# Turning eight kept rows of h by transposing DMAs instead of on TensorE, with a new order of all instructions

## The chip, the cores and the metric

The kernel runs on one core of a Trainium2 chip. The metric is the device time of one execution in microseconds (us); a time "of the runs" is the median of separate executions. One execution was also recorded by the hardware profiler, and everything said of engines, waits and transfers comes from that record. Engines are named as the profile names them: PE (TensorE: matmuls and transposes), DVE (VectorE), ACT (ScalarE), POOL (GpSimd) and SP (the engine that issues the DMAs here).

## The reference

A layer with a forward pass and its gradients, in bfloat16, with S = 2048 tokens, D = 512 channels and F = 1376 hidden features. Cut to what matters:

```python
xn  = layernorm(A_q)
kv  = shift_conv(k, shift_k) * v                  # four taps along the tokens
y   = causal_conv(kv, ssm_k) + kv * ssm_D         # convolution over all 2048 tokens, by FFT
mlp = ((xn @ w_gate) * (xn @ w_up)) @ w_down      # no nonlinearity: a bilinear GLU
out = A_q + xn * y + mlp
# result: out, and the gradients of out with respect to A_q, k, v, shift_k,
# ssm_k, ssm_D, w_gate, w_up, w_down for the given grad_out
```

With g = xn @ w_gate, u = xn @ w_up and d = grad_out @ w_down^T, the bilinear part needs three products per token and hidden feature: g·u (for the output and for w_down's gradient) and d·u, d·g (for the gradients of w_gate, w_up and xn). In the kernel these three are called **h**. Each h is needed twice and in two layouts: with tokens on the partitions for the weight gradients, and with features on the partitions, that is transposed, for the output and for the gradient of xn.

## The kernel before, in words

**Tiling.** The 2048 tokens are R = 16 rows of 128 tokens. Features are cut into NST = 6 stages j of 256 columns, stage 1 being only 96 wide (L26). `mlp_rows` (L402) makes h for one stage and two rows: matmuls into PSUM, copies by ACT and DVE, and products by DVE. It writes them to a ring in SBUF of RING = 28 slots; a slot of 1536 bytes per partition holds the three h of one row and one stage, that is 128 partitions by 768 bf16 values. `slot(j, r)` (L273) gives the address. Stage 4's rows 0 to 15 lie in slots 0 to 15 and stage 5's in 16 to 27 and 0 to 3.

**From rows to features.** `hd_store` (L429) stores h to a DRAM tensor HD, and `hd_load` (L616) later loads one pair of rows back through a transposing DMA, into one of two buffers of SBUF, `hdP[n % 2]`. It is one DMA per row pair n = 0 to 7: 1152 rows by 768 columns for n < 4 and 896 rows by 768 columns for n = 4 to 7. The second is smaller because the last KEEP = 8 rows of stage 4, like all 16 rows of stage 5, are never stored: they stay in the ring ("kept rows") and are turned in place. `turn_gen` (L593) does that: 24 kept rows of 6 blocks of 128x128 each are 144 transposes on PE, eight at a time into PSUM, and each eight are copied back over the slot by one ACT COPY of 128x1024. `hd_block(m, t, fb)` (L620) tells the matmuls where the transposed block fb of row m lies: in a loaded buffer or in a ring slot.

**Stages of time.** The MLP stages run first, together with `dw_gen` (L568: the weight gradients of a finished stage, matmuls over its ring rows) and `a_gen` (L439: first step of the long convolution). Then `s_gen` (L550) does the middle of the convolution through the DRAM tensors AX and CX, beside the last weight gradients. From about 275 us on comes what is called the **F part** here, a loop over the eight row pairs n: `c_load` (L650) brings 1.5 MB of CX, `last_dft` (L691), `c_dkv`, `c_y`, `c_o5`, `c_dsk` and `dk_pair` finish the convolution and its gradients, mostly on DVE; `y_o` (L756) and `y_x` (L773) are the groups of 11 and 22 matmuls of 128x512 per row that read the transposed h and give the output and the gradient of xn. `hd_load(n + 2)` fills the buffer that the groups of pair n read last.

**Order.** Nothing runs in the order of the Python text. Every call on an engine is recorded as an operation (the helper at L173 then issues it, so that nearly every instruction of the profile has the line L173), and `emit` (L181) replays them in an order unpacked from the string PLAN, which also names a PSUM bank for every buffer. This string sets each engine's order, and SP's: all DMAs are issued from SP into one hardware queue, in PLAN's order. An SP instruction that waits holds up all DMAs behind it. The DMAs share eight semaphores in turn, so that each also waits for the one eight places before it.

Of the kernel before, what the change touches and what calls it, by code (L numbers as in the profile page):

```python
# [10 lines left out]
BF = mybir.dt.bfloat16  # L11
# [6 lines left out]
S = 2048  # L18
D = 512
F = 1376  # L20
R = 16
NFB = 11
NST = 6
# [5 lines left out]
KEEP = 8  # L29
RING = 28  # L30
RO = [0, 16, 24, 40, 56, 72]
EPS = 1e-5
PLAN = "c-lQzbrhFHu$`WzyBq0lBn0Ucl<rOmLFtwTC8a?^q`O1u?v@To=|(}~{qVi>&bPbY?CjlhXXc-sn-Kt#07EfI0P!IyB!qY%P!tkDW+)B{1`fF(86<`PQ6MVhhG-BSQov^r15!auNDi?eHXwWsai9d0f;><fN<vD=52>L5bb`205XwOrNCV}eEL4EJ@F^66e9!<sf$H!K3d3{w3K~H*aIFC~p$Qa$T2KdCLuY6SJ)sRWgvwAGDneuE4RxUxjDc401q_Bt&=l%HCYTIEpbw0KW>6m%LthBm7Dhuq7z<rs0BnKg@HO;@b}$9T!4mi$+Cvri76!sr=m1$@5Uhi}kQUNIM_2><AS+abTsR(P!#6M$et~o_4Ss_4uok|9=`aE2z+A`)8z47sgyFCWy21$P26^yTm;sxiJ4}S3Fb@{Mm+%`*f}deN41-&c3SYtt$cw+jD;Nn&VL2>=g)kE`z~8U}Rzfs92#a7p`~%w{A0C1O@B{3C!|)nX<4(8$X>dCnfozZ#Kfz0o1M=f8NQZA=H=Kl3kRCH&Mmz=aFcY4Jb5H=^!f`kcXW$~7fPWz~{sEUE3!a7BkQM)g=y)As;0<^W*)Tiagkz8ct7A?qh&Aw2tcil}pb*By!dMGyV=TM_vGEGjLB%3i7Y&PIJ*<z8E#NPRgG+G<eul+x85YL|_&I)n78n=fV@tdWt#CQ6hA6lKTVoqUY>N#M@Gk7YuW=<d!eQ7B+aqBIY>dNk72bm%Apv&8Z?F?a#YET{o8V5|g$Z#tHpOqT8ScRmxEB-SefSQiVOM+rBa!h3d<fleH8#he@JAelQ}7Y2#V0TtyWlu{3^Q;#PQdZF27kuxxCp1>7#xceu_R8y9#{hRVRq<=y)X%`!&2BAH(+Tz3WKN&_QAerx)J+ffBXdp(*RtLzv68C9_QdpyiILr2+hTSWpN-L#CbRf=VLi6j|*@cwxyvoj0WQnOp3{II90&Lv>#_-GOUPAsUc0J5j2esU<zzTm2f(>qDIt&T2pgcj4kMEYDb-^2OPq0X$DosqxcPdfj`q>tb#{yCRN2Ru@ilTDRCAZ$7+~}64M#{1J7a-`kv0=dAxuZF)1aZOL!TR(-mw_SMeJDiL>b>rl9M13V);<*nn>0LOeyc@HXDTzwj=0pp-O_PT)OEMW^XLo}tu~h92NUe1wnj4|;-|@hLvTp?H>_;}(2@FYy)rjcMs0e2s7LUz`PR@g2U$4+wOEkUpW`Fdd~Qq71|&q|}EBQAMgmg((vmITfLzl$qvGpvshmveG%qMxRj>ib};O8WpFEbPPYI67&UCp{n#HeMKdy6qTmF6rHM38Hz!_V|E%z=P4#tryLZE%2I6FgmLHx+K%NYF2$pqv=#4AeEN%OP%g?%lj$xcpz?GYCu1JUOZliK)uP%|hw4%V%1`&G9?hi!RFFQU?`R&)rykUWex+X2jk?k*>P<aq6s@K))Sp(+SXxgTX%F<Hm9&gT(+0Xvn`kYKr{%PUcF|9?nI_T>x=7>bH=01ZX$ozlowSg)(|cM%59keDgGsc7_R=D{K#OS){Y!7@cltnw=^dS<Kj{eVC*&J+lLk;sK0piT5nU(XhZLJ*@l!ZRariMEq9?@sl(te%&c)9tHy@>?B%FtjQC`l+m*^_x=POizFH=GOl$`??;==rbUQtR;#YMO%f5v~)Eh@$@DK$T*=zNWoV{kkk$BEduI7j7wC@x3gk^BQE;h~&>6LV4?&QUZCkKm}9kcaU;O3rEdM@~qiI2nJ!#OZiEm*6S<6PM(vJdLaIbgs_nIRj_pOgw>Wa9oY2@pT6O%q=N1N7I@-iED9mjiE7h442|8oRv#+EFH_)IJRcz+FXX`aao?o2{ew*<-}Tt%W--Bh3ZoUuE>eBBmK%rwJzu2N}N!WXcw->$+a@q=lT2vXVtFUjjM12&Ze&^nWoU}no?8i9Inb=a$5b0b7*(Ypba^l{=%uW5$Do0nqGTwPVLE`Xk*T;y|@WC<viM(7jj0O#m%@6_vO5rS^IH+E~J?>i#F#0{5`keQd&e?ax2cK3%IZj<j;8!7u9t%nAdYjEvBt`1GnL}{58+y&$N~<;o4eO+i`xaqf5Cx7tqqWj63kB+L60c8Lgltw4kQoa#~3nXnFmHmvcjHq#L;tU*pcag8$^}TwK4<P5doa)s<XVzvCNxlPhX<ea5%AvewhD^h>?X&-o75)E4>|*Vnt;Qa{(#e2-W0eSW|Xxs^WRD*Bi^YEyl}jr9dr(;E7%HrJQ@iqlI5$tcaVwRY0u)Ir;5CizC=^LLtAhVa+=H+RwB_#b}FUA3FG*DTUj+v)e(L*MWq%_>dwUw+F2wX<fE?DCF>>3bfbJNN_VkZlZ-Q*uc(9<JSWu=dh^x|311a~~b5xn+R%)-60ldn!p^9jT+akZk4Myo(D<9vP!WWHI;GsX9gT$_y<iV>O?Q(_?&`i^_QYRPxJOUdNxwPdY(Q@JZgxKkHImuH|Hzp5oK|qn_bExV%i)X*x=0X)zhCGxaR*=h=FY5AZoY#6Rc?U8(V9j#iRibd^?+^L&Ia@LXN3lewZy*0p+(FY#W!%#~%LuF-j#Kv;g&gtABzNn%-`3w0ka(cQX1CutQ)BC|QEh!mGix>2w2dQB#aHMv~nEt*0Ob6wf1^YwE%sM|E9Y}GGho$k{5l1l2yW^Ev;Mdf!*Bc&v*{HBNX6WOCBq_phUbh1wm=w&S_NA-|4l0AG?O|EEdDI?ppj<{UV9eP}Y9MMZ!Riem6J)y_+tTvRga!R90G&!y3^eLaw^IBcLk{WVdtI0{dp=-FiT+^HSrSy<?(puWfEp020^o~ZCo>Eg{$RB!JW6BeaC9&nPzR;cewX~6^`cnVWT5?xk=~3<_%_WZ9(~i<qddo8<Yaz`fuKcObmEa$3EMoVyk93f}@<#uZe!><{u8Ud|`CDJB+k5?2`^#0iCO2e&nElSdZpu@MVqhQi8@VmF<eh#mZ#9uU(1FrY21!&yi*DaZD|se^C59!jnATZ_NEi85;#y+sB#-5e#J3OfMB-UDS;R?gs1%T{azsFfNi2(F(d?ndwxe=iQdn~POO8n@yDO*<WSZo#ly*;YT0%>0&t<y2kX)9`j>`#|AzAHbNo(2cq@=T%a!O818vDc&*h85m*)6?gv<ya?*>c+%$!oJEk3Ev&_J^F6b8=qtSqaNztof~g&5;Z8i_Ddaa!Cr>uad>)$*1<Y&6fqTP!>rcyKiOep<R}e_F78Yzw*Eq%kT153fpkmB4w?djga#8w-mLJ@`DtyA7zw`maS6E#>i*3O~y(^D`n$kygauG_JwVi%J!2~vI(+7zO;!lNhZrTwo`UV6?-F7WVckaS|(c6mPj4@NA}2G*(dwufE<)Va#%W9XIm;?*)o|bwXLo#mwL8BUdgw%QtI1x*2SvZOIanWrK@$bnzlyvS$C^pbFGoRu*SAl8d?)uC;P2|HMM58UN*=(X>L92iEWgg_Qnp_3F~F=<yU)bo8*WcwBGi}`q(^cVMk51ueG#RHs6j}YinZ*Y`krjw${(SwsyAA7THPr$tGBP>u(dSgZ(Cx?6^&~j<(pA*c4l8FHQW4Otob;&8FLOTVd|6>~DK*-`fluXkYnL8x)aJKigo7<1_6a`(Q(Ct<AEPHq@f{FjJpx>uiqwVux(Kt+Lg2*f!X3dv7Cbr2SwUZIeB-%@+KW{b&R1HydSZESjIT-))PHHukNy&BoYv8*4jkr;W2+h92E_+a62hF+8=ui?mreJdMZn{BEAi|FyJ!*<$+{`@@oZ0#E1#JcXz9PrRBJ^mM-0u2?pIYl%FuC-GQb*gy63UePOgQjhA@J*Q{zhF-*r`e&Zq3wbdw?zugm$Mri_!}IuAtKdz&rZ@A?{i6M4xx9pz^t@ihdwXdw<>#%8SN3>b%lmj|KWBZtqkreMy}8%%3)aaqd3mqv8NG$~^UU7O%X&S};@^5puj*O7zW4VpeSlxG2L7j&^Dlh7fA5XFyI;2+-pYURZ@j0s_PO5J+xXZ1t9S7qe4aP)uHMVr`cFR6fAsi1*eCc3Z|CiOmCyGDKGR3}T^s0we1tFbi9Xub`xu|(8+?&Z_TPMn->{+nyN~m+zQwotYM<gAe3(!5n>NiC`!-+W+kLn%@vFAccldO_XPbPfFY|Ri%V+pO|Ji5zHT%b3`y1csyZw}J_O<@6FZY#x$glfh-{pJ!hM)9ze%kl?F@NS4{HD+GeSXF-`XBz>ulOxL;!pjoKlT^?-p~05Kkk?Or9-&wcYMDe@DqO7F<f;DfBAX;G~D%1!u?3AXW^cw3vXS5hC<<idng?K^uIlNNFT0w{BYEZgohqNh7d1g3<<&`&lF;WgyEIP44K0dj}nrFL?L-d6{3b{Aw`H25{J)1l8`ba4fR9!kS`Ps#X{<kCFBpqL*9@zd>(RzG@(Su7D|R5p?Sy?VukFXMJN^0hDsrJ$Psde8liOP8OnsXp=`(<dWCYKL8u<ehlZhMs1OQ<mZ5T}6<URgp;2fZYKJ!Ai_kWF9SVdhp<U<@`h>4S-%uyC5B);j&@nU)T|$#kHS`ZnL#Hqx)C=E*Z$q`vEZnm1!_+V^{1C>4X<<&dZG*!2FgOeeL&Gm&SePE>hF`<H@Kg9E%n0+t?yw*X4?l*5VM6E{7KMpnRM-=K4ogDsus4hiox|cVDeMcY!_u%aEDIyT{xCU=3<tuL@E{xvXT!O0KFkcW!^7}pcoZIoC*e>y5@v<NVO>}sj)o24Sm+i;hYMk2SQ9pd<6(1n8ZL%Q;aS)gR)ycf+Hg6%48MnW;d$5|u7nriS{M_qhFf8ISP|ZbSK-faGwcW_!j^C{d<fUWo3Jz74*!N5VQct1+zGqFsqi-Z6aESi<#f0kUWYT`Uic&24`}8D#G($&WXO@nOq38jqRU)`-ARCj%$da^^36Uj5fnP$M_ZY|Bany}ATmGx#SI9>B0U+HAw)1HAI~gu9}E!PK2i#T(f>LlLtK^AFv4mY;ShyLKyDlf4OmshkSNj*f&xY;BS4GvE|D<)GyWUu5f8cGN7Excfhur>F%rgqGZJG&asqu!BSIZ%B|fs7M81!E`*`vZ5CMKn<v%>Z|L*_a`_Yn*Mfks45Ya~wu^TBKT7(}N5ZEKz|1yhUI8tOml8?1SSN>QE_eds@HBu+|Siwj_ALX&5qWb>;ZQ!K("
KB = 1024


# [1 line left out]
def kernel(  # L38
# [31 lines left out]
    HD = dram.tile([R, 640, 768], BF, name="HD")  # L70
# [7 lines left out]
    Q = [PP[:, 1024 * i:1024 * i + 1024] for i in range(4)]  # L78
# [130 lines left out]
    ldT = nc.sync.dma_start_transpose  # L209

    def place(shape, dt, at):
        n = 1
        for s in shape[1:]:
            n *= s
        if dt == BF:
            v = big[0:shape[0], at // 2:at // 2 + n]
        else:
            v = big[0:shape[0], at // 2:at // 2 + 2 * n].bitcast(dt)
        if len(shape) == 3:
            return v.rearrange("p (a b) -> p a b", a=shape[1])  # L220
        if len(shape) == 4:
            return v.rearrange("p (a b c) -> p a b c", a=shape[1], b=shape[2])
        return v
# [18 lines left out]
    RH = 34 * KB  # L242
# [7 lines left out]
    W2 = W12[:, 128:192]  # L250
# [22 lines left out]
    def slot(j, r):  # L273
        return RH + 1536 * ((RO[j] + r) % RING)
# [11 lines left out]
    kh = ra.tile("kh", [128, R + 3, D])  # L286
# [57 lines left out]
    n0 = [0]  # L344
# [221 lines left out]
    f = {}  # L566

    def dw_gen(j):  # L568
# [21 lines left out]
            ACOPY(v3(dwx[:, 2 * fw * q:2 * fw * q + 2 * fw], 2), pw)  # L590
        st(ow[:, WO[j] + 4 * fw:WO[j] + 12 * fw], dwx[:, 0:8 * fw])

    def turn_gen():  # L593
        for j, r0 in ((NST - 2, R - KEEP), (NST - 1, 0)):
            blk = [(r, t, b) for r in range(r0, R) for t in range(3) for b in (0, 128)]
            for k in range(0, len(blk), 8):
                pt = bfv(rN(), 8, 128)
                for i, (r, t, b) in enumerate(blk[k:k + 8]):
                    nc.tensor.transpose(pt[:, i, :], ring(j, r)[:, 0, t, b:b + 128], ident[:])
                r, b = blk[k][0], k % 6  # L600
                ACOPY(place([128, 8, 128], BF, slot(j, r) + 256 * b), pt)
                yield
# [17 lines left out]
    def hd_block(m, t, fb):  # L620
        h = hdP[m // 2 % 2]
        a = hd_span(m // 2)[0]
        if fb == 10:
            return h[:, 3 * (m % 2) + t, 512 - a:640 - a]
        if fb >= 8 or fb >= 6 and m >= R - KEEP:
            return place([128, 6, 128], BF, slot(fb // 2 + 1, m))[:, 2 * t + fb % 2, :]
        c = hd_at(fb // 2, m % 2) - a
        return h[:, 2 * t + fb % 2, c:c + 128]

# [418 lines left out]
```

## Time and profile before

| | |
|---|---|
| median of three runs | 430.09 us (427.62 to 433.96) |
| profiled execution | 429.69 us: span 427.9 us and 1.8 us around it |
| granted PE clock in it | 1.00 |
| PE busy | 418.4 us, 98% |
| DVE busy | 352.5 us, 82% |
| ACT busy | 268.3 us, 63% |
| DMA queue of SP | 124.13 MB, 89.7% of the 16 DMA engines' time |
| PE transposes and warm-ups of 128x128 | 216 |
| transposing DMAs from HD | 8 |

Busy time is the time in which an engine has an instruction of its own in work. The span begins with the first and ends with the last instruction. "Releaser" in a view is what ended an engine's wait. In a view of groups, `xN` counts instructions, the number behind the bar is busy time, then the mean ns of one, then idle time before the group and what ended it. In a view of windows, each row gives a stretch of the span, its length, busy time and instruction count of PE, PE's weight loads, DVE, ACT and POOL, the granted clock, the DMA engines' busy share and GB/s. That share is made by adding up the packets of all queues and can exceed 1.

### The profile page before, as it was taken

The page shows a single profiled execution, that of the slowest core. Times are in us where ns is not written, and L with a number is a line of the kernel's source. Part 1 is how long each engine was busy: PE and PEld are TensorE (multiplying, and loading weights), DVE is VectorE, ACT ScalarE, POOL GpSimd, SP SyncE. Part 2 cuts the span into 40 slices and gives each one's busy share as a digit, 9 for nine tenths or more (in the row PEclk, how much of TensorE's full clock was granted, in tenths as well). Part 3 has the DMA queues.
Part 4 walks back from the last instruction along what each step waited for, and adds up shares of the span by engine and source line. Part 5 has one row for each costly group of instructions (what it writes and reads, how often), then busy time and mean ns, then how long its engine had stood idle before and what let it go on. Part 6 is the DMA issues. An engine that isn't in the chain of part 4 may idle for free.

```text
span 427.9 us, 8313 instructions
## 1 busy us (share of the span) xinstructions
PE 418.4 (98%) x3270; PEld 203.4 (48%) x3270; DVE 352.5 (82%) x684; ACT 268.3 (63%) x374; POOL 3.4 (1%) x9
## 2 busy tenths in 40 slices
PE   7999999999999999999999999999999999999996
PEld 4655455755453343443444344444444434444443
DVE  4989989978649889999999991055857999999997
ACT  4895879698644899898998957554343342214333
POOL 1000000000000000000000001000000000000000
PEclk9999999999999999999999999999999999999999
DMA  7994798979777789985978988999999999999935
GB/s 245 396 409 163 253 330 293 402 286 382 290 247 258 234 333 306 359 318 196 347 256 354 337 243 295 228 336 367 273 254 318 285 304 345 289 316 263 247 98 193
DMA packets 94622, 124.64 MB, mean 291 GB/s; under 512 B 53492, under 2 KB 63609, under 8 KB 93560
## 3 DMA queue, kind: packets, MB, share of 16 engines
q1 hardware_dynamic: 94584, 124.13, 89.7%
q8 instruction: 25, 0.41, 0.4%
q14 instruction: 13, 0.11, 0.1%
HBM read 57.10 MB, written 54.04 MB: 260 GB/s over the span
## 4 chain that ended last, share of the span: by engine, by line
PE 76%; DMA 12%; DVE 7%; SPq 3%; issue 1%; ACT 1%; DVEq 0%
PE PP L173 76%; DVE big L173 7%; DMA out_dram<-big 3%; DMA big<-HD 3%; SPq L173 3%; DMA big<-in_x_dram 2%; DMA big<-AX 2%; DMA big<-in_w_dram 2%; ACT big L173 1%; DVEq L173 0%
## 5 line engine op out<-in xcount | busy, mean ns | idle before, releaser
L173 PE MATMUL PP<-big 128*128 128x512 bf16 (+8 forms) x3270 | 418.4, 347 | 5.3 <-DVE big L173 2.6
L173 PEld LDWEIGHTS <-big 128*128 128x128 bf16 (+4 forms) x3270 | 203.4, 97 | 219.8 <-issue 62.3
L173 DVE TENSOR_TENSOR big<-big 128x1024 bf16<-128x1024 bf16 (+4 forms) x465 | 269.2, 630 | 37.4 <-ACT big L173 22.7
L173 ACT CAST big<-PP 128x1024 bf16<-128x1024 f32 (+2 forms) x314 | 225.8, 779 | 86.3 <-PE PP L173 64.1
L173 ACT ACTIVATE big<-big 128x512 bf16<-128x512 f32 (+3 forms) x30 | 18.9, 642 | 46.0 <-DVE big L173 45.8
L173 DVE CAST big<-PP 128x512 bf16<-128x512 f32 (+1 forms) x37 | 32.2, 874 | 16.8 <-PE PP L173 12.1
L173 ACT COPY big<-PP 128x1024 bf16<-128x1024 bf16 x25 | 25.2, 1015 | 20.5 <-PE PP L173 20.4
L173 DVE SCALAR_TENSOR_TENSOR big<-big 128x1 f32<-128x1 f32 (+2 forms) x52 | 25.2, 499 | 0.3
L173 DVE TENSOR_TENSOR big<-big,PP 128x512 bf16<-128x512 bf16 x14 | 9.5, 682 | 10.2 <-PE PP L173 10.1
L173 DVE BATCH_NORM_STATS2 big<-big 128x6 f32<-128x512 bf16 x16 | 10.4, 680 | 3.7 <-DMA big<-in_x_dram 3.7
L173 DVE SCALAR_TENSOR_TENSOR big<-big,PP 128x512 f32<-128x512 bf16 x14 | 9.6, 682 | 0.3 <-PE PP L173 0.2
L173 DVE TENSOR_SCALAR big<-big 128x1 f32<-128x1 f32 (+1 forms) x28 | 7.0, 257 | 0.3
L173 POOL MEMSET big<- 128x1536 bf16 (+2 forms) x3 | 2.8, 949 | 258.7 <-DMA big<-in_sk_dram 258.7
L173 DVE RECIPROCAL big<-big 128x2 f32<-128x2 f32 (+1 forms) x9 | 1.4, 158 | 2.4 <-ACT big L173 2.4
L173 ACT ACTIVATE big<-PP 128x512 f32<-128x512 f32 x2 | 1.2, 597 | 2.6 <-PE PP L173 2.6
L173 DVE BATCH_NORM_AGGREGATE big<-big 128x2 f32<-128x6 f32 x16 | 2.2, 164 | 0.1
L173 ACT ACT_TABLE_LOAD x1 | 1.3, 1283 | 0.7 <-PEq L1036 0.7
L173 DVE DVE_READ_ACCUMULATOR big<-big 128x1 f32 x16 | 1.3, 82 | 0.0
L173 DVE DVE_READ_ACCUMULATOR big<-big,PP 128x1 f32 x14 | 1.1, 82 | 0.0
L173 DVE MEMSET big<- 128x128 bf16 (+1 forms) x2 | 0.2, 112 | 0.8 <-PEq L1036 0.8
L173 DVE COPY big<-PP 128x1024 bf16<-128x1024 bf16 x1 | 0.7, 655 | 0.0
L173 ACT ACTIVATION_READ_ACCUMULATOR big<-PP 128x1 f32 x2 | 0.4, 194 | 0.0
(6 smaller groups left out, 0.9 us busy)
## 6 DMA issues: line engine op xcount, KB each, us to landing
HD<-big SPq DMA_DIRECT2D x32, 384.0 KB, 6.2
AX<-big SPq DMA_DIRECT2D x16, 768.0 KB, 5.8
big<-AX SPq DMA_DIRECT2D x16, 768.0 KB, 6.7
CX<-big SPq DMA_DIRECT2D x16, 768.0 KB, 4.9
out_dram<-big SPq DMA_DIRECT2D x44, 256.0 KB, 4.0
big<-CX SPq DMA_DIRECT2D x7, 1536.0 KB, 7.9
big<-in_v_dram SPq DMA_DIRECT2D x16, 256.0 KB, 6.3
big<-in_w_dram SPq DMA_DIRECT2D x4, 768.0 KB, 7.2
```

The source lines that it names most:

```text
L173: o.fns.append(lambda: f(*[fix(x) for x in a], **{kk: fix(x) for kk, x in k.items()}))
```

## The change

Of the 24 kept rows, the eight of stage 4 (rows 8 to 15) are no longer turned on PE. Four transposing DMAs, one for two rows, read their ring slots in SBUF and write the transposed blocks to ring slots again, shifted down by four: rows 8 to 15, in slots 8 to 15, go to slots 4 to 11. The first of the four (rows 8 and 9) overwrites the slots of stage 4's rows 4 and 5, which are read last by the weight gradients of stage 4; each later one overwrites slots which an earlier turn, or the weight gradients, has read. `hd_block` reads these eight rows from the shifted place. The sixteen rows of stage 5 are still turned on PE.

PLAN is another string, so that the order of every engine, the places of all DMAs on SP and the PSUM banks differ throughout. In the new order the turn of rows 8 and 9 stands on SP behind the last store to CX and before the last quarter of `c_load(0)` and `hd_load(0)`. Those of rows 10, 12 and 14 stand directly behind `hd_load(5)`, `hd_load(6)` and `hd_load(7)`.

```diff
--- before.py
+++ after.py
...
-PLAN = "..."
+PLAN = "..."
...
+    BYDMA = 4
+
+    def by_dma(j, r):
+        return (r - R + KEEP if j == NST - 2 else KEEP + r) // 2 < BYDMA
+
+    def turned(j, r):
+        return RH + 1536 * ((RO[j] + r - 4 * by_dma(j, r)) % RING)
+
     def turn_gen():
         for j, r0 in ((NST - 2, R - KEEP), (NST - 1, 0)):
-            blk = [(r, t, b) for r in range(r0, R) for t in range(3) for b in (0, 128)]
+            for r in range(r0, R, 2):
+                if by_dma(j, r):
+                    ldT(out=place([128, 12, 128], BF, turned(j, r)), in_=place([128, 1536], BF, slot(j, r)))
+                    yield
+            blk = [(r, t, b) for r in range(r0, R) if not by_dma(j, r) for t in range(3) for b in (0, 128)]
             for k in range(0, len(blk), 8):
                 pt = bfv(rN(), 8, 128)
                 for i, (r, t, b) in enumerate(blk[k:k + 8]):
...
         if fb >= 8 or fb >= 6 and m >= R - KEEP:
-            return place([128, 6, 128], BF, slot(fb // 2 + 1, m))[:, 2 * t + fb % 2, :]
+            return place([128, 6, 128], BF, turned(fb // 2 + 1, m))[:, 2 * t + fb % 2, :]
```

In the code, by_dma also has a case for stage 5; with BYDMA = 4 it is never true there, since KEEP + r is at least 8.

## The prediction

> **What bounds the kernel now.** I read the totals first, then the chain that ended last, then the stretch that holds the change. In the totals PE is busy nearly all the time, and the second half of the DMA row is nines:
>
> ```profile
> PE 418.4 (98%) x3270; PEld 203.4 (48%) x3270; DVE 352.5 (82%) x684; ACT 268.3 (63%) x374; POOL 3.4 (1%) x9
> DMA  7994798979777789985978988999999999999935
> PE 76%; DMA 12%; DVE 7%; SPq 3%; issue 1%; ACT 1%; DVEq 0%
> ```
>
> The third line is the chain's shares: PE 76%, DMA 12%, DVE 7%. Its pieces (start, length, what), of which these carry the reading:
>
> ```profile
> 139.37 135.29 PE PP L173 x1303
> ...
> 293.80 13.47 DMA big<-HD
> ...
> 307.31 4.32 PE PP L173 x36
> ...
> 346.86 52.00 PE PP L173 x292
> ...
> 401.77 6.68 DVE big L173 x13
> ```
>
> Up to 275 us PE alone sets the pace. In the F part the chain also runs through the transposing loads from HD (293.80) and at the end through DVE. The windows of the F part (start:end, length, busy PE, PEld, DVE, ACT, POOL, clock, DMA share, GB/s) show three engines full at once:
>
> ```profile
> 282.00:291.00 9.00, 8.88 (x66) 4.03 (x64) 3.62 (x6) 5.77 (x8) 0.00 (x0) 1.00 0.99 356
> 299.00:306.00 7.00, 7.00 (x57) 2.97 (x56) 5.21 (x9) 1.93 (x2) 0.00 (x0) 1.00 1.29 235
> 351.00:371.00 20.00, 20.00 (x117) 8.86 (x116) 19.67 (x42) 5.47 (x6) 0.00 (x0) 1.00 1.12 310
> ```
>
> The DMA share is about 1 from 271 to 404 us; the packets leave only some 3.5 to 4 us without traffic in these 133. So PE sets the end, but a microsecond taken from PE is paid in a currency, DMA time, that is scarce exactly where three of the four new transfers stand.
>
> **What goes.** 48 transposes and six ACT copies:
>
> ```profile
> L173 PE MATMUL PP<-big 128*128 128x128 bf16 x216 | 16.4, 221 | 0.6 <-DVE big L173 0.5
> L173 ACT COPY big<-PP 128x1024 bf16<-128x1024 bf16 x25 | 25.2, 1015 | 20.5 <-PE PP L173 20.4
> 265.80:266.69 0.89, 0.89 (x17) 0.88 (x16) 0.00 (x0) 0.23 (x1) 0.00 (x0) 1.00 1.01 286
> ```
>
> Of the 216, 144 turn kept rows. The 221 ns is the length of one in the pipeline, not what it costs: in the window two groups of eight pass in 0.89 us, 55.6 ns each from start to start. PE loses 48 × 55.6 = **2.67 us**, all of it from 262 to 281 us, where the chain is on PE. The copies (6 × 1.015 = 6.1 us of ACT) are worth nothing: ACT is 63% busy and waits for PE.
>
> **What is added: four turns.** No SBUF-to-SBUF transpose runs before, so I bound it. The HD loads as the tile's view has them (issue time on SP in ns, min/median/max), and in time on SP:
>
> ```profile
> L173 SPq DMA_TRANSPOSE big<-HD x8: 8065/8429/9878, 269.9 to 391.7; - x8
> ...
> 326.32 8.63 SPq L173 DMA_TRANSPOSE big<-HD  x1
> ```
>
> In the packet records a load of 1152 rows is 6912 packets of 256 bytes and holds the DMA engines 7.7 to 8.25 us; one of 896 rows is 5376 packets and 6.0 to 6.7 us. The difference, 1536 packets for about 1.6 us, is just one turn (128 × 1536 bf16 values, 0.39 MB); by the mean rate of 1.13 ns per packet a turn takes 1.75 us. Against this, SP's issue time does not shrink with the size (8.06 to 8.50 us for the smaller loads too, since SP is held by the backlog), and nothing shows that reading from SBUF partitions is as quick as from HD. The ends: 0.3 us, the issue of a plain 256-KB transfer, and 8.06 us, the cheapest HD issue. I take **1.75 us of the DMA engines and 2 us of SP**, the row with the same kind and packets.
>
> [...]
>
> **Does each turn fit?** The first (rows 8, 9) stands behind the last CX stores. Before, SP waits there from 263.5 to 269.46 us for a CX store to land; the turn lies in that wait and costs nothing up to about 5 us. What it writes over was read by weight gradients that end three PE operations after the last `s_Bi`, so it waits for nothing new. Behind it on SP are the last quarter of `c_load(0)` and `hd_load(0)`.
>
> The others stand behind `hd_load(5)`, `(6)`, `(7)`, where the buffer's hand-over is the tight place. Before, PE had 12.2, 14.8 and 13.7 us of work between the last reader of the old buffer and the first of the new; the loads landed 12.05, 13.75 and 13.4 us after that last reader. Adding up the durations of before in the new order, the turned blocks are first needed 15.7, 16.5 and 17.0 us after release. With 2 us for the turn they land at 14.05, 15.75 and 15.4: margins of 1.65, 0.75 and 1.6 us. Queued behind the turns on SP are stores, `y_load`, `k_load` and `c_load`; SP waited 39.8 us for PE in six places between 311 and 407 us, so 2 us there come out of waiting. Cost: **0**, thinly. Without that cover each turn would cost up to its 2 us.
>
> **What the new order moves.** Two places lose. (1) Before, 14.34 us passed from the start of the last `s_Bi` (260.47) to the first `last_dft` (274.81), while its chain of CX store, CX load took 13.34 (landed 273.81). The new order has 12.9 us of PE work there: a stall of **0.4 us**. (2) The second pair's load landed at 307.26 and was used at 307.31. In the new order two or three more 256-KB transfers (0.6 to 0.7 us each) stand between `hd_load(0)` and `hd_load(1)`, and PE is there 0.4 us earlier: up to **2 us** of stall; below, 0, if these fit into the gaps of the DMA engines. I take 1.
>
> Two places gain, as cover. Hand-overs of pairs 2 to 7 are wider than the tightest before (15.65, 16.6, 15.7, 13.9, 14.8, 16.1 us against 12.2 to 14.8), and PE's work behind the first use of pair 7 falls from 17.97 to 15.59 us, so a late last load costs 2.4 us less.
>
> **Sum**, against the profiled execution's own 429.69 us (0.4 below the median of the runs): 429.69 − 2.67 + 0.4 + 1.0 = 428.4. I forecast **428.5 us**, practically no change; its own range is 425 (no stall, and a somewhat better order) to 432 (the full 2 us, and two of the thin margins gone). About 2% is what a measurement of this kernel can tell from no change.
>
> **Rivals.**
> *A, a turn is as dear as a whole HD load* (8.2 us, on SP and on the engines). For it: SP's issue time did not follow the size, and the source is 128 partitions instead of DRAM. Against it: engine time followed the packets. Each of the three hand-overs would be late by 8.2 − 2 less its margin: 4.55, 5.45 and 4.6 us. The backlog that delays the loads (2 to 4.5 us from issue to first packet) would shrink while PE waits, so I take 9 to 14.6 of these 14.6 us. The first turn would hold `c_load(0)` 2.5 us longer. 428.4 + 2.5 + 9 to 14.6 = **440 to 445 us**, slower. It begins to tell at 2.75 us per turn (the margin of pair 6) and passes 2% at about 5 to 6 us. [...]
>
> *B, everything added is hidden*, both stalls too: 429.69 − 2.67 = **427.0 us**, down to 425 with the wider hand-overs. For it: PE waits only 0.2 us for HD in all of before. Against: the full DMA engines.
>
> *C, the saving does not reach the end*, since the DMA stage sets it: four turns are 7 us of engine time, the gaps 3.5 to 4, so the last HD load lands up to 3 us later (404.94 to 408), with 2.4 us less work behind it: 429.69 + 3 − 2.4 = **430.3 us**, and 429 to 431.5 if one us more or less fits into the gaps.
>
> **Chances.** The forecast 0.37, B 0.14, C 0.21, A 0.22, and 0.06 for losses of the new order of 9 us and more that I do not see: DVE is 98% busy from 340 us on, and any late pair shifts all of its work. Faster by over 2% would need 421 us, 6 us more than PE loses: 0.04, taken from B. So faster 0.04, same 0.68, slower 0.28. The range is 425 to 442: it leaves out the lower edge of B and the upper half of A.
>
> **What would show it.** In the changed profile the 128x128 matmuls should be 168 instead of 216 and the copies of 128x1024 19 instead of 25. Four DMA_TRANSPOSE big<-big should stand on SP with about 2 us each (8 us: rival A). PE's waits should name HD once, at pair 1 (0 to 2 us), CX once (0.4 us), and the turned tile never; waits of 4 us and more at pairs 5 to 7 mean A. For C the last HD load lands at 406 us or later with PE waiting there. The forecast is wrong if a turn holds SP over 2.75 us, or if DVE, waiting for late pairs, ends past 428 us.

## The result and the profile after

Over 22 runs each, the changed kernel takes 428.10 us (426.60 to 429.22) and the kernel before 429.16 us (427.62 to 433.96). The ratio is 0.9967 with a 95% interval of 0.9952 to 0.9983: 1.4 us faster, 0.7 to 2.1 by the interval, far within 2%. The profiled execution took 428.71 us (span 426.9) against 429.69.

The totals of the changed kernel, the DMA row and the chain's shares by engine, as the page has them:

```profile
PE 416.2 (97%) x3222; PEld 200.3 (47%) x3222; DVE 352.4 (83%) x684; ACT 261.3 (61%) x368; POOL 3.5 (1%) x9
DMA  7995979988888779977978998999999999999954
PE 64%; DVE 16%; DMA 15%; issue 2%; SPq 1%; ACT 1%; ACTq 0%; DVEq 0%
```

PE has 2.2 us less to do and DVE as much as before. The chain runs less through PE (76% before) and more through DVE and DMA. The two groups that were to shrink, in the view of groups by form:

```profile
L173 PE MATMUL PP<-big 128*128 128x128 bf16 x168 | 12.3, 220 | 0.8 <-DVE big L173 0.7
L173 ACT COPY big<-PP 128x1024 bf16<-128x1024 bf16 x19 | 18.8, 1021 | 8.2 <-issue 5.7 <-PE PP L173 2.4
```

They shrank by 48 transposes and six copies. On SP, in order of time, the four turns (start, time on SP, what) and the tile's view of the HD loads:

```profile
261.96 3.32 SPq L173 DMA_TRANSPOSE big<-big  x1
...
367.48 2.65 SPq L173 DMA_TRANSPOSE big<-big  x1
...
385.38 1.48 SPq L173 DMA_TRANSPOSE big<-big  x1
...
403.22 1.50 SPq L173 DMA_TRANSPOSE big<-big  x1
```

```profile
L173 SPq DMA_TRANSPOSE big<-HD x8: 6994/8163/10565, 267.0 to 393.0; - x8
```

A turn holds SP for 1.5 to 3.3 us, not for the 8 us of an HD load. The first stands free in the packet records: its 1536 packets pass from 265.64 to 267.99 us, 2.35 us. The windows that were shown of before:

```profile
282.00:291.00 9.00, 9.00 (x72) 3.83 (x70) 3.81 (x6) 6.97 (x10) 0.00 (x0) 1.00 1.02 379
299.00:306.00 7.00, 6.32 (x73) 3.40 (x72) 5.21 (x14) 3.35 (x4) 0.00 (x0) 1.00 1.25 250
351.00:371.00 20.00, 20.00 (x117) 8.91 (x116) 18.33 (x39) 5.26 (x6) 0.00 (x0) 1.00 1.12 298
```

The DMA engines are as full as before. New is the 0.7 us that PE lacks from 299 to 306. Where PE waits in the F part, in PE's view in order of time (start, length of the busy stretch, what it begins with, and in brackets the wait ahead of it and its releaser):

```profile
301.08 5.76 PE L173 MATMUL PP<-big 128*32 128x512 bf16 x78 [0.68 <-DVE big L173]
308.20 88.09 PE L173 MATMUL PP<-big 128*128 128x512 bf16 x523 [1.36 <-ACT big L173]
397.36 1.57 PE L173 MATMUL PP<-big 128*128 128x512 bf16 x12 [1.06 <-DVE big L173]
399.10 23.64 PE L173 MATMUL PP<-big 128*32 128x512 bf16 x143 [0.17 <-DMA big<-CX]
```

The same view of PE's weight loads has, at the second of these places:

```profile
308.20 15.65 PEld L173 LDWEIGHTS <-big 128*128 128x128 bf16 x74 [1.53 <-DMA big<-HD]
```

The wait at 308.20 is the first use of pair 1: `hd_load(1)` landed at 308.16. The matmuls' view puts the wait down to ACT, where an instruction happened to end at 308.17; no output matmul needs it, and the weight loads name HD. From there PE runs 88 us without a gap.

**Where the time went.** Starts on PE, before and after: the first `last_dft` at 274.81 and 271.78 (3.0 us earlier); pair 1's first output matmul at 307.31 and 308.20; pair 5's at 370.83 and 370.87; the end of PE at 423.7 and 422.7. So 3 us were won, nothing is left of them at pair 1 and at pair 5, and 1.0 us comes back behind pair 5. From the first `last_dft` to pair 1 the changed kernel takes 3.9 us longer. Of these, 2.2 us are PE work that the new order does earlier (PE busy 34.4 us against 32.2) and 1.7 are waits (2.0 against 0.3). Behind pair 5, PE has 2.2 us less to do (50.6 against 52.9) and waits 1.2 us longer. So it is open whether the 1.0 us at the end is "2.7 us of PE less the stalls", as the prediction has it, or the work of the new order. The experiments are about this question.

### The profile page after: what moved, and what is told of

The parts are those of the page before. It is cut to its first block, busy times and chain, and to the rows that moved or that the text cites. A ratio compares the mean times of both kernels' runs of the same rounds, so it can differ in the third digit from the quotient of the medians.

```text
span 426.9 us, 8210 instructions
## 1 busy us (share of the span) xinstructions
PE 416.2 (97%) x3222; PEld 200.3 (47%) x3222; DVE 352.4 (83%) x684; ACT 261.3 (61%) x368; POOL 3.5 (1%) x9
## 4 chain that ended last, share of the span: by engine, by line
PE 64%; DVE 16%; DMA 15%; issue 2%; SPq 1%; ACT 1%; ACTq 0%; DVEq 0%
PE PP L173 64%; DVE big L173 16%; DMA out_dram<-big 6%; DMA big<-in_k_dram 4%; DMA big<-in_tab_dram 2%; DMA big<-AX 2%; SPq L173 1%; DMA big<-in_goT_dram 1%; ACT big L173 1%; DMA HD<-big 1%; ACTq L173 0%; DVEq L173 0%
## 5 line engine op out<-in xcount | busy, mean ns | idle before, releaser
L173 PEld LDWEIGHTS <-big 128*128 128x128 bf16 (+4 forms) x3222 | 200.3, 97 | 221.9 <-issue 63.9
L173 ACT CAST big<-PP 128x512 bf16<-128x512 f32 (+2 forms) x314 | 224.9, 780 | 114.1 <-PE PP L173 82.8
L173 ACT COPY big<-PP 128x1024 bf16<-128x1024 bf16 x19 | 18.8, 1021 | 8.2 <-issue 5.7
L173 DVE BATCH_NORM_STATS2 big<-big 128x6 f32<-128x512 bf16 x16 | 10.3, 678 | 3.3 <-DMA big<-in_x_dram 3.3
```

Of the source, the lines that this page charges most:

```text
L173: o.fns.append(lambda: f(*[fix(x) for x in a], **{kk: fix(x) for kk, x in k.items()}))
```

## Experiments

Two theories. **T**, the prediction's: PE bounds the kernel, its saving counts wherever it lies, and the turns are hidden. **C**, its third rival: transfers bound the F part, and PE's saving does not arrive. Ratios are to the kernel before, run beside each kernel on the same chip. Some records of matmuls are missing in the traces of the experiments, so starts on PE were read from the weight loads, which are complete. A profile is one execution each; two of the same kernel differ by about 1 us in where things stand (the changed kernel's pair 5 starts at 370.87 us in one profile and at 369.84 in another).

### The old order, without and with the turns

```diff
 for i in order:
+    if i in left_out:      # six groups of transposes and their copies, stage 4
+        continue
```

> The old order without the six groups of transposes and the six copies for stage 4's rows 8 to 15 (these rows are left unturned, so this part of the computation is missing), and without any DMA in their place. It prices the PE term alone. If the end follows PE, as the prediction has it: 2.7 us faster than before (ratio 0.994). If the DMA stage or DVE, both full from 340 us on, sets the end whatever PE saves at 262 to 281 us (rival C): no change, ratio 0.998 to 1.000.

430.98 us, ratio **1.0037** (1.0015 to 1.0059): slower, though PE has 2.67 us less to do. Where PE waits now:

```profile
271.70 31.76 PE L173 MATMUL PP<-big 128*32 128x512 bf16 x229 [1.45 <-issue]
304.02 2.89 PE L173 MATMUL PP<-big 128*128 128x512 bf16 x24 [0.56 <-DMA big<-HD]
...
324.35 1.48 PE L173 MATMUL PP<-big 128*32 128x512 bf16 x24 [0.79 <-DMA big<-CX]
...
331.50 13.04 PE L173 MATMUL PP<-big 128*128 128x512 bf16 x94 [1.23 <-ACT big L173]
346.66 78.53 PE L173 MATMUL PP<-big 128*128 128x512 bf16 x438 [2.12 <-DVE big L173]
```

The first of these lines is the first `last_dft`: the last quarter of `c_load(0)` landed at 271.61 us, and PE, with less to do ahead of it, stood waiting for 1.45 us. So more than half of the 2.67 us is lost at once, to a transfer. PE reached pair 2 3.3 us earlier than in the profile of before (320.05 against 323.34; 2.4 us of that lead stood already at 146 us, ahead of anything that was taken out). It had given all of it away by 360 us. The window behind the longest wait shows a further loss, the granted clock of 0.50 ahead of the DMA share:

```profile
347.30:350.70 3.40, 3.40 (x10) 1.19 (x9) 3.26 (x5) 0.81 (x1) 0.00 (x0) 0.50 1.26 225
```

From the end of that wait to pair 4 PE takes 13.34 us here (346.66 to 360.00), and 11.65 us (347.33 to 358.98) in the run with the fill below, where the clock stayed at 1.00: the half clock cost 1.69 us of PE.

```diff
 for i in order:
     if i in left_out:
         continue
     ...
+    if i is hd_load(n), n = 4 to 7:
+        turn rows 2n, 2n + 1 by a transposing DMA
```

> The old order, the same six groups taken out, and the four turning DMAs put behind the HD loads of pairs 4, 5, 6 and 7: the change without a new order. If the turns hide in the hand-overs even here: as the old order without turns, ratio 0.994 to 0.996. If the new order's wider hand-overs are what hides them: the tightest hand-overs of before had 0.15 to 1 us to spare, so up to 2 us lost at each of pairs 5, 6 and 7, in all 3 to 5 us above the old order without turns, ratio 1.000 to 1.006.

437.29 us, ratio **1.0187** (1.0147 to 1.0226), 6.4 us above the old order without turns, more than either line expected. That is 1.6 us per turn, where a turn's packets take 1.8 to 2.9 us in this profile, so most of it shows. Compare the new order:

### The new order, with none, and with more turns

```diff
+left_out = the four turning DMAs
```

> The changed kernel without its four turning DMAs (the rows stay unturned, so this part of the computation is missing). By the prediction the turns are hidden: the same time as the changed kernel, ratio to before 0.995 to 0.997. If the DMA stage sets the end (rival C), 7 to 9 us of transfers less give 1.5 to 4 us: ratio 0.987 to 0.993.

427.14 us, ratio **0.9949** (0.9929 to 0.9970). Beside 0.9967 for the changed kernel the four turns cost about 0.8 us, which the intervals do not separate from nothing. T's reading of the turns holds, and the new order is what makes them affordable. C had expected 1.5 to 4 us here. Three of the four turns stand behind the HD loads of pairs 5, 6 and 7, so that at most the last part of the F part could feel them.

These ratios split the change. Taking the transposes off PE in the old order cost 1.6 us (1.0037). The new order, with no turns at all, is 3.8 us faster than the old one, with no turns at all (0.9949 against 1.0037). The four turns cost 0.8 us. The sum is the 1.4 us that were measured. No run has the new order with the transposes still on PE, so what their removal is worth in the new order alone stays open.

```diff
 ldT(out=turned(4, r), in_=slot(4, r))
+ldT(out=slot(4, free), in_=slot(4, r))     # r = 10, 12, 14; free = 8, 4, 6
```

> The changed kernel with each of the turns of rows 10, 12 and 14 issued a second time, into ring slots that are dead by then. The margins worked out in the prediction (1.65, 0.75 and 1.6 us) are then passed by 0.4 to 1.5 us each: 1 to 4 us slower than the changed kernel, ratio to before 0.999 to 1.006. If DMA engines are the bound throughout (rival C): the whole 3 times 2.2 us, ratio 1.010 to 1.013. If the margins are wider than worked out: no change, ratio 0.997.

436.17 us, ratio **1.0153** (1.0119 to 1.0186): 8 us above the changed kernel for three turns more, 2.7 us each, above C's whole price. PE's waits from pair 5 on:

```profile
380.52 1.91 PE L173 MATMUL PP<-big 128*32 128x512 bf16 x32 [1.74 <-DVE big L173]
...
390.35 7.29 PE L173 MATMUL PP<-big 128*128 128x512 bf16 x32 [0.46 <-DMA big<-HD]
400.12 1.57 PE L173 MATMUL PP<-big 128*128 128x512 bf16 x12 [2.47 <-DVE big L173]
403.17 2.75 PE L173 MATMUL PP<-big 128*32 128x512 bf16 x24 [1.49 <-DVE big L173]
```

These are 6.2 us of waits where the changed kernel has 1.2, and the clock was at half from 401.6 to 408.4 us. The margins of 0.75 to 1.65 us in the prediction were used up by the first set of turns; the second set pays in full, and the clock adds to it.

### Is it the clock, or DVE?

```diff
+# ahead of the first matmul of y_x(3, 0), in the old order without turns
+8 x matmul(psD, lhsT=zero, rhs=go[:, 0, :], start=False, stop=False)
```

> The old order without the stage-4 turns once more (1.5 us slower than before, although PE has 2.7 us less to do), with eight matmuls of zeros, 1.7 us, added in the place where PE waits 2.1 us for DVE at 346 us (ahead of the first gradient matmuls of row 6); they add zero to the sum that gives the gradient of shift_k. Its profile showed half the granted clock for 3.4 us right behind that wait, which costs 1.7 us. If the wait is what lowers the clock, filling it keeps the clock at 1.0 there: 1.7 us faster than without the fill, ratio to before 0.999 to 1.001. If the half clock is an accident of that execution or does not set the end: ratio 1.003 to 1.005.

430.89 us, ratio **1.0040** (1.0009 to 1.0071): no change. The fill did what it was made for, as the same window shows:

```profile
347.30:350.70 3.40, 3.37 (x16) 1.56 (x16) 3.23 (x7) 0.82 (x1) 0.00 (x0) 1.00 1.22 226
```

And in PE's view there is a wait at pair 5 that was not there without the fill:

```profile
372.48 52.68 PE L173 MATMUL PP<-big 128*128 128x512 bf16 x306 [0.75 <-DMA big<-HD]
```

The clock stays at 1.00, and pair 4 starts at 358.98 instead of 360.00. But pair 5 starts at 372.47, against 372.30 without the fill: PE now stands waiting for `hd_load(5)`, which landed at 372.43. The granted clock of whole executions agrees: without the fill it was 0.994 to 0.996 in five of twelve, as one stretch or more at half clock make it, and with the fill in one of twelve. Without the fill those five took 430.2 to 432.5 us and the other seven, at 0.998 and more, 429.4 to 432.4. So the half clock went with the wait, 2.12 us without the fill and 0.19 with it, and it still was not what set the end. That is evidence for C.

```diff
+left_out = the seven DVE operations of dk_pair(4)
```

> The changed kernel without the seven DVE products and sums of one dk_pair (rows 4 and 5, 4.8 us of DVE at about 350 us; the gradient of k for these rows is not computed, its store stays). If DVE, busy without a break from 340 us on, sets the end of the changed kernel: 3 to 5 us faster, ratio to before 0.985 to 0.990. If the hand-overs of the HD buffers or PE set it, as the prediction's steps assume: less than 1 us, ratio 0.995 to 0.997.

427.89 us, ratio **0.9974** (0.9949 to 0.9999): the same as the changed kernel. 4.8 us of DVE (4.2 by DVE's busy time in the profile) are worth nothing, though DVE has 16% of the chain. A place on the chain that ended last is no proof of a bound where several engines end nearly together.

### The late load of pair 1

```diff
 # SP's order (numbers count SP's DMAs in the changed kernel)
-182 dks copy, 183 k_load, 184 o5 store, 185 KS load, 186 dks copy, 187 hd_load(1)
+183 k_load, 185 KS load, hd_load(1), 182 dks copy, 184 o5 store, 186 dks copy
```

> The changed kernel with hd_load(1) moved ahead of three of the five DMAs in front of it (the store of o5 of pair 1 and two copies of dks), so that it no longer has to wait for c_load(2), the DMA eight places before it. It is then issued up to 4 us earlier. If the wait of 1.4 us at pair 1 is the loss that the prediction put at 0 to 2 us, and it is owed to this place in the queue: 0.7 to 1.5 us faster than the changed kernel, ratio to before 0.993 to 0.995. If the transfers in front, not the place, set its landing, or if the later stage gives the lead back: no change, 0.996 to 0.998.

429.98 us, ratio **1.0026** (0.9998 to 1.0054): 2.5 us slower than the changed kernel. The load came 5 us earlier (issued at 290.64, landed at 303.02 instead of 308.16), and PE lost more just before it:

```profile
305.38 22.40 PE L173 MATMUL PP<-big 128*128 128x128 bf16 x152 [2.91 <-ACT big L173]
```

ACT's copy of o5 for pair 2 overwrites the buffer that the store of pair 1 reads. That store now stood behind `hd_load(1)`, which held SP for 10.3 us; ACT's copy started at 304.31 instead of 302.65, and PE waited for the PSUM behind it, then ran 3.4 us at half clock. Neither line of the expectation had this: I had moved a store without asking who waits for its buffer.

```diff
-182 dks copy, 183, 184, 185, 186 dks copy, 187 hd_load(1)
+183, 184, 185, hd_load(1), 182 dks copy, 186 dks copy
```

> The changed kernel with hd_load(1) moved ahead of only two copies of dks on SP; the store of o5, whose buffer ACT waits for, stays where it was. hd_load(1) then lands some 4 to 5 us earlier, as in the run before, and ACT is not held up. If the wait for HD at pair 1 is what the changed kernel loses of PE's gain: 1 to 1.5 us faster than the changed kernel, ratio to before 0.992 to 0.994. If the chain of HD and CX loads behind it gives the lead back: 0.996 to 0.998.

429.82 us, ratio **1.0001** (0.9982 to 1.0021). Issued 5.6 us earlier, the load lands at 307.50, only 0.7 us earlier:

```profile
291.25 12.71 SPq L173 DMA_TRANSPOSE big<-HD  x1
```

SP is held for 12.7 us instead of 7.7, so that 5.0 of the 5.6 us go into the hold. So the place eight behind `c_load(2)` did not set its landing; that the transfers in front did, the second line of the expectation, is the reading that is left. The kernel is about 1.2 us slower than the changed one beside it, with intervals that overlap. Why was not settled; PE's waits in its profile are at pairs 1, 5, 6 and 7, the longest 1.57 us at pair 7.

### What bounds the F part

```diff
 for fb in range(NFB):
     MM(po[:, c], lhsT=hd_block(2 * n + rr, 0, fb), ...)
+    if n == 2 and 1 <= fb <= 9: left out
```

> The changed kernel without 18 matmuls of 128x512 of the output of rows 4 and 5 (feature blocks 1 to 9 are left out of these rows' output), 3.9 us of PE between 321 and 340 us. If PE bounds the F part of the changed kernel, since it stands still nowhere from 308 to 396 us: 3 to 3.9 us faster, ratio to before 0.987 to 0.990. If the chain of transfers is a bound of equal rank (HD loads land 0 to 0.3 us before PE uses them at pairs 5 and 6): 0 to 1.5 us, ratio 0.993 to 0.997.

429.02 us, ratio **0.9975** (0.9951 to 0.9999): 3.9 us of PE (3.4 by PE's busy time, against the profile of the control) are worth nothing in the new order either. The control beside it:

> The changed kernel as it is, beside the two above: ratio to before 0.996 to 0.998.

428.74 us, ratio **0.9973** (0.9949 to 0.9998). The profile without the 18 matmuls shows where they went:

```profile
340.27 15.83 PE L173 MATMUL PP<-big 128*32 128x512 bf16 x88 [2.48 <-DMA big<-CX]
...
372.26 10.65 PE L173 MATMUL PP<-big 128*128 128x512 bf16 x71 [0.98 <-DMA big<-HD]
...
400.38 1.48 PE L173 MATMUL PP<-big 128*32 128x512 bf16 x24 [1.23 <-DMA big<-CX]
```

The three longest waits from 309 us on are all for transfers. The first two, 3.5 us together, took up what was saved; in the place of the third the control waits too, 1.70 us for CX. Now the transfers, taken away where nobody waits for them:

```diff
 st(o2[...], acc)      # dk_pair
+left out for r0 = 2 to 10
 st(o5[...], o)        # c_o5
+left out for n = 2 to 6
```

> The changed kernel without ten stores of 256 KB in the F part (the gradients of ssm_k for pairs 2 to 6 and of k for rows 2 to 11 are computed but not stored), at 0.7 us of the DMA engines each some 7 us of transfers on which no other work waits. If the transfers set the end of the changed kernel, as the run with less PE work says: 2 to 4 us faster than the changed kernel, until PE, which waited 3.3 us after 270 us, is the bound; ratio to before 0.988 to 0.993. If neither transfers nor PE but the fixed order of waits sets it: 0.996 to 0.998.

425.93 us, ratio **0.9918** (0.9887 to 0.9949): 2.2 us below the changed kernel, inside what C expects. One wait of PE of over 0.3 us is left from 270 us on:

```profile
306.79 17.98 PE L173 MATMUL PP<-big 128*128 128x512 bf16 x104 [1.15 <-DMA big<-HD]
```

> Both: without the ten stores and without the 18 matmuls (3.9 us of PE). If transfers and PE are bounds of equal rank, so that PE's saving shows once the transfers are out of its way: 2 to 4 us faster than with fewer stores alone, ratio to before 0.979 to 0.988. If transfers bind even with ten stores fewer: the same as with fewer stores alone.

425.35 us, ratio **0.9895** (0.9849 to 0.9942), not separable from fewer stores alone. Its profile, an execution of 427.21 us, says where the 3.9 us went there: they end in one wait for `c_load(4)` (landed at 339.65, in the changed kernel at 340.32):

```profile
339.69 2.57 PE L173 MATMUL PP<-big 128*32 128x512 bf16 x25 [2.50 <-DMA big<-CX]
```

and the window behind it is at half clock:

```profile
340.60:343.80 3.20, 2.98 (x17) 0.94 (x11) 2.78 (x6) 2.31 (x3) 0.00 (x0) 0.50 1.00 335
```

The six executions fall into two groups. Three with a granted clock of 0.999 to 1.000 took 422.9 to 424.2 us, and three with 0.995 to 0.996, like the profiled one, 426.5 to 427.8. Where the clock held, PE's saving does show, about 2 us below fewer stores alone, as "bounds of equal rank" expected. That is three executions, sorted after the fact, and so a hint and not a proof.

**The chain of transfers, side by side.** All times in us, from SP's order and the landings, PE's by its weight loads:

| kernel | PE starts `last_dft(1)` | `hd_load(4)` issued | `c_load(5)` issued, landed | `hd_load(5)` issued | PE starts pair 5 |
|---|---|---|---|---|---|
| before | 287.56 | 343.31 | 352.57, 360.20 | 360.27 | 370.83 |
| old order, no turns | 283.90 | 342.53 | 352.51, 360.53 | 360.60 | 372.30 |
| changed | 284.77 | 341.86 | 351.60, 360.07 | 360.13 | 370.87 |
| changed, less PE | 284.71 | 341.70 | 352.43, 361.68 | 361.74 | 372.26 |
| changed, fewer stores | 284.31 | 340.06 | 348.27, 356.29 | 355.83 | 369.45 |

In the first four rows PE enters the F part up to 3.7 us earlier or has less to do, and `hd_load(5)` goes out at 360.1 to 361.7 us all the same. In these rows it is issued 0.06 to 0.07 us after `c_load(5)` has landed, since that one stands eight places before it and shares its semaphore; `c_load(5)` is issued when SP is through with `hd_load(4)` and two or three DMAs of 256 KB; `hd_load(4)` holds it for 8 to 9 us (8.06 before, 8.05 in the changed kernel). There is no PE in this stretch of the chain. One load further back there is: in the changed kernel `hd_load(3)` went out at 323.52 us, 0.02 us after PE released its buffer, while in the kernel before it followed the landing of the DMA eight places before, by 0.07 us.

In the row "old order, no turns" the load itself landed at 370.14, 2.2 us before PE used it: PE came late by its own waits and the half clock, and only with the fill did it meet the load.

Only the row with fewer stores moves the chain, by 4.3 us. There PE is the bound again: `hd_load(5)` landed at 366.64, 2.8 us before PE used it. The 1.4 us at pair 5 are not owed to the stores, though. PE was that much earlier already at pair 1 (306.79 against 308.20), ahead of the first store that was left out, and ran without a gap from there to pair 5 in both. What the stores gained lies behind pair 5, where PE takes 50.3 us to its end instead of 51.9 and no longer waits 1.06 and 0.17 us. Fewer DMAs also change which one stands eight places before another: `hd_load(5)` is no longer tied to `c_load(5)` here, and went out 0.02 us after PE released its buffer. The run does not separate the lighter traffic from these other ties.

In the changed kernel the two bounds meet: `hd_load(5)` landed at 370.77, and PE, without a gap since 308, was there at 370.87.

## Why the prediction was right, and which steps were not

The time (428.5 forecast; 428.10 measured, and 428.71 in the profiled execution that the sum stands for), the sign and "within 2%" came out. The steps fared differently.

- **The PE term** had the right size: PE busy fell by 2.2 us, and `last_dft(0)` starts 3.0 us earlier (0.8 of it because PE's wait for AX was shorter in this execution, 0.51 against 1.30). But "all of it where the chain is on PE", so that it counts in full, was wrong as far as the runs show. The old order without the transposes gained nothing, 1.45 us of it going at once into a wait for `c_load(0)`, and 3.9 us taken out later in the new order gained nothing either.
- **The failed step is the first one: what bounds the kernel.** "PE sets the end" let every microsecond of PE count. From pair 1 on PE and the chain of transfers are bounds of nearly equal rank, and a saving on one alone stops at the other: 3.9 us of PE gave nothing, ten stores less gave 2.2 us. Rival C had the saving that does not arrive, at a chance of 0.21. Its time, 430.3, was a miss for another reason: it let the four turns push the last HD load up to 3 us later. That load landed at 405.27 us, against 404.94 before, and PE did not wait for it. With 0.3 us in place of 3, C's sum gives 427.6. The 3 us were what was left of 7 us of turns after gaps of 3.5 to 4 us without traffic; counting every packet to its end, the kernel before has only 0.3 us of such gaps. Why the old order without the transposes is 1.6 us slower, and not merely as fast as before, stays open: its longest waits are for DVE and ACT, and filling one of them changed nothing.
- **What the new order gains**, which the sum left out: it brings 2.2 us of PE work forward from behind pair 5 to ahead of pair 1. Of these, 1.2 were lost again in waits at pairs 6 and 7 (1.06 for DVE, 0.17 for CX; the weight loads have 0.23 for HD and 0.21 for the turned rows besides), and 1.0 us arrives.
- **The turn's size** was 1.75 us on the engines and 2 on SP; measured 2.35, and 3.32, 2.65, 1.48, 1.50. Rival A, 8 us, is out. The row with the same packets was the right one to go by, but the first turn took 34% more: 1.53 ns per packet here, where the HD loads of the same profile take 1.04 to 1.19 when they stand alone. The spread is wide: in the other profiles of the new order the first turn's packets take 2.1 to 3.4 us, and in this one the last turn's, behind `hd_load(7)`, 1.96. The sign "wrong if a turn holds SP over 2.75 us" was met by the first turn, 3.32, but there SP would have waited anyway; in the three tight places it was not. (That SP's issue time "does not shrink with the size, 8.06 to 8.50 for the smaller loads too" left out the last of these four, 9.64.)
- **The first turn in SP's wait for CX**: it cost nothing, as worked out, and SP still waited 1.26 us for the CX store after it. The reading behind it was too wide: before, SP issued two loads from 263.58 to 266.13 us and waited only from there to 269.46. The turn fitted because these loads do not stand there in the new order.
- **The stall at c_load(0)**, 0.4 us, did not come: from the store's issue to the load's landing passed 9.9 us instead of 10.7, and PE was at `last_dft(0)` 0.4 us after it.
- **The stall at pair 1**, 1.0 with 0 to 2: 1.4 us measured. The reason given, the transfers in front, is the reading that the second of the two runs on it leaves. At 301.08 another 0.68 us were lost that the prediction had not.
- **"Cost 0, thinly"** for the other turns: about 0.8 us for all four. Thin is confirmed, for a second set cost 2.7 us each. But the margins were counted from the hand-over of the buffer by PE, and none of the three loads went out on it: `hd_load(5)` followed the landing of `c_load(5)`, by 0.06 us, and `hd_load(6)` and `hd_load(7)` the DMA ahead of them on SP, by 0.09.
- **The shorter tail**: from pair 7's first use to PE's end 18.5 us before and 16.2 after (17.97 and 15.59 counted).

Two errors went in opposite directions: the PE term was counted on a path that, by the runs, it does not reach, and the gain behind pair 5 was left out of the sum, though both figures of the tail stood in the text as mere cover. That the forecast came within 0.2 us of the profiled execution is therefore partly luck. The profile alone would not have told: up to its end PE is busy 2.2 us less and idle 1.2 us more than before, which reads like the sum's −2.67 and +1.4. Only the runs that took work out show that what PE alone saves is taken back by new waits.

Of the versions that do all of the work, none is faster than the changed kernel.

## What to carry to other kernels

Where two resources are full at once, ask of each saving what the other one does in the meantime: here the DMA chain from `hd_load(4)` through the queue to `hd_load(5)` contains no PE at all, and the quickest test is to take work out of each in turn (PE, DVE, transfers) and see which moves the end. An order that is searched for a kernel fits that kernel: the same removal of 2.7 us cost 1.6 us in the old order, and four such DMAs cost 6.4 us there and 0.8 in the new one. Before a store is moved behind a long transfer, look up who writes its buffer next.

## What the runs showed of the hardware

**The clock after a wait.** PE's longest waits in the F part of the profiles, and the granted clock behind them: after 1.91 us (new order, no turns), 2.12 (old order, no turns), 2.47 (three turns more), 2.50 (fewer stores and less PE), 2.52 (old order with the turns) and 2.91 (`hd_load(1)` early, the first of the two) it went to 0.50 for 3.4 us (for 6.8 us with three turns more, where a second wait of 1.49 followed); after one of 2.48 us (changed, less PE) it did not, nor after one of 1.96 us far ahead of the F part, at 10 us; after those of 1.74 (three turns more), 1.81 (old order with the turns) and 1.84 (the fill) and all shorter ones it stayed at 1.00. So half the clock followed six of these eight waits of 1.9 us and more. What it cost beyond the wait itself was measured twice: 1.69 us in the old order without turns, as above, and 1.69 us in the new order without turns, where PE's 104 recorded matmuls from the wait at pair 1 on take 19.67 us (306.85 to 326.52), against 17.98 (307.18 to 325.16) in the control of the changed kernel. The kernel before has no wait of a matmul over 1.30 us, and the changed kernel none over 1.36 in one profile and 1.70 in the other; the granted clock of these three profiles is 1.00, 1.00 and 0.999.

**A transposing load from HD held SP for 7.0 to 10.6 us** in the profiles of before and of the changed kernel, while its packets took 5.6 to 8.3 us. The same load, `hd_load(1)`, held SP for 7.7 us in the changed kernel and for 12.7 when it was issued 5.6 us earlier, and landed only 0.7 us earlier. So SP's time in this load did not follow from its size alone. In the changed kernel the three turns directly behind a load held SP for 2.65, 1.48 and 1.50 us, and the one behind stores for 3.32.
